# Two reorderings in the attention part of a fused attention and MLP kernel: row maxima four heads ahead instead of three, and the memory's update before its reads

## The chip, the cores and the metric

The kernel runs on one core of a Trainium2 chip. The metric is the device time of one execution in microseconds (us). Three runs of the kernel before gave 2224.09, 2224.89 and 2230.13 us; the median is 2224.89.

A core has five engines that run side by side, each in the order of its own instruction list: PE (matrix multiply; the profile shows its weight loads apart, as PEld), DVE (vector), ACT (activations and copies), POOL (GpSimd) and SP, which here does nothing but issue DMAs. An engine stands still when its next instruction waits for a semaphore, and everything behind that instruction in its list stands with it.

## The reference

The block is a conditioned residual pair: `x + ga * A(h)` with attention A, then `x + gb * B(h)` with a token-mixing MLP B. Only A matters here: 2048 rows in 4 segments of 512, 32 heads of width 32. Each segment attends to itself under a causal mask, and also reads a memory that earlier segments have filled:

```python
for s in range(N):                       # 4 segments
    qs, ks, vs = q[:, :, s], k[:, :, s], v[:, :, s]
    logits = jnp.einsum("bhqd,bhkd->bhqk", qs, ks) * scale + mask
    p = _softmax(logits, axis=-1)
    a_dot = jnp.einsum("bhqk,bhkd->bhqd", p, vs)
    pq = phi(qs)
    num = jnp.einsum("bhld,bhde->bhle", pq, M)
    den = jnp.einsum("bhld,bhd->bhl", pq, z)[..., None] + 1e-6
    o = g * (num / den) + (1.0 - g) * a_dot
    pk = phi(ks)
    M = M + jnp.einsum("bhld,bhle->bhde", pk, vs)
    z = z + jnp.einsum("bhld->bhd", pk)
```

All of it is in float32 accuracy: large products are made from operands that are split into a high and a low part, three matmuls for one.

## The kernel before, in words

**Units of work.** The attention is cut into 32 iterations t: group g of four heads, segment seg, in the order `its`: first segments 0 and 1 of every group (t = 0 to 15), then segments 2 and 3 (t = 16 to 31). An iteration has four heads h, so there are 128 heads, numbered n = 4t + h.

**The loop.** One pass of the loop at line 686 belongs to one n and records pieces of several iterations: the `scores` of head n, the row `maxima` of the head that is LEADS = 3 further on, the `values` of the head two back, and one of four pieces of `project` for the iteration two further on (LEADP = 8 heads). Into it are planned the loads and splits of the next group's weights, eight more x tiles (`token_tile`), 32 parts of the modulation matrix (`mod_fetch`, `mod_late`: a load "rawm" and one long DVE operation, L573) and wo.

**One iteration.** `project` makes k and v of the segment (matmuls `nps`, L192), transposes k (`kps`), makes q (`qps`, L200), splits k and q into high and low parts ("sg") and sends them by three small DMAs a head into that head's stack "sk" (`stack`, L374 to L376). Its last piece makes v's parts and calls `memory`. `maxima` multiplies q and k of a head (`sx`, `sy`, `sz`, L478), DVE takes the masked row maxima (L480), and for every second head PE transposes the eight columns (`nmps`, L486), ACT and DVE split them ("nt"), and four DMAs write the negated maxima of a pair of heads into rows 96 and 97 of their stacks (L493). `scores` can start only then: its matmuls `a0`, `a1`, `a2` (L515 to L522) use all 98 rows, so that the maxima are subtracted inside the product. ACT takes the exponentials (L516, L519, L523), POOL masks the diagonal blocks (L526), ACT casts a float16 part (L528), POOL makes the rest (L530), and `values` multiplies both with v (`pv`, L544). After the fourth head PE transposes the output (`ops`), ACT copies it ("ot"), and a DMA stores it ("oT").

**The memory.** `memory` (L441) reads M and z of the group (one tile MZ) in two halves: matmuls `rd` (L450), then three DVE operations (L452 to L454) that write half of tile "am". Then it makes the update: matmuls `up` (L460), DVE's masked product (L465) and POOL's sum into MZ (L466). The bank of PSUM (PE's output memory) that all these use, "ms", exists once, and `nmps` and `ops` use it too: whoever comes next waits until the one before has been read out.

**What sets the order.** The lines only record work. A scheduler of the language then places the instructions on each engine's list, after its own estimate of a timeline, within the limits of data, of buffers (banks "s1" for maxima, "s2" for scores and "pj" for projections exist twice, "pv" and "ms" once) and of `issue_after`. So a changed place in the code moves instructions nearly everywhere in the attention part. SP has one list for all DMAs, in the scheduler's order.

After the attention come the output projection (`po`, L791) and the MLP (`mx`, L921).

Of the kernel before, what the change touches and what calls it, by code (L numbers as in the profile page):

```python
# [18 lines left out]
P = 128  # L19
# [10 lines left out]
LEADP, LEADS, NSK = 8, 3, 8  # L30
# [8 lines left out]
LEADS = 3  # L39


def attention_and_mlp(ctx, tc, x, wq, wkv, wo, beta, w1, b1, w2, b2, c, wm_a, wm_b, out):
# [29 lines left out]
    def bank(tag, bufs, name):  # L72
        return psum.tile([P, 512], F32, tag=tag, bufs=bufs, name=name)
# [304 lines left out]
    def project(t, piece):  # L378
# [50 lines left out]
        else:  # L429
# [9 lines left out]
            memory(t)  # L439

    def memory(t):  # L441
        pr, g, seg = its[t]
        d = st[t]
        d["am"] = am = b.tile([P, 4, 128], F32, tag="am", bufs=3, name=f"am{t}")
        if seg:
            for half in range(2):
                ps = bank("ms", 1, f"rd{t}_{half}")[:, 0:264].rearrange("p (a n) -> p a n", a=2)
                for aa in range(2):
                    i = 2 * half + aa
                    T.matmul(ps[:, aa], d["pq"][:, 128 * i:128 * i + 128], MZ[:, g], start=True, stop=True)  # L450
                rd = b.tile([P, 2, 4], F32, tag="rd", bufs=2, name=f"rdd{t}_{half}")
                V.tensor_scalar_add(rd, ps[:, :, 128:132], 1e-6)  # L452
                V.reciprocal(rd, rd)
                V.tensor_tensor(am[:, 2 * half:2 * half + 2].rearrange("p a (h e) -> p a h e", h=4),  # L454
                                ps[:, :, 0:128].rearrange("p a (h e) -> p a h e", h=4),
                                rd.unsqueeze(3).to_broadcast([P, 2, 4, 32]), op=ALU.mult)
        if seg < 3:
            ps = bank("ms", 1, f"up{t}")
            for i in range(4):
                T.matmul(ps[:, 0:132], d["pk"][:, i], d["v32"][:, i], start=(i == 0), stop=(i == 3))  # L460
            if seg == 0:
                V.tensor_tensor(MZ[:, g], ps[:, 0:132], bdg[:, g], op=ALU.mult)
            else:
                tm = b.tile([P, 132], F32, tag="tm", bufs=1, name=f"tm{t}")
                V.tensor_tensor(tm, ps[:, 0:132], bdg[:, g], op=ALU.mult)  # L465
                G.tensor_tensor(MZ[:, g], MZ[:, g], tm, op=ALU.add)  # L466
# [126 lines left out]
    def at(f, n):  # L593
        if 0 <= n < 4 * NI:
            f(n // 4, n % 4)
# [90 lines left out]
    for n in range(-LEADS, 4 * NI + VL):  # L686
# [9 lines left out]
        if m >= 8:  # L696
            at(project, m)
        if 59 <= m < 67:
# [442 lines left out]
```

## Time and profile before

| what | us |
|---|---|
| median of three runs | 2224.89 |
| the profiled execution, its own time | 2226.6 |
| its span, first to last instruction | 2224.9 |
| PE busy in the span | 2190.3 |
| DVE / ACT / POOL busy | 1666.7 / 1135.7 / 725.8 |
| mean granted PE clock | 0.997 |

The attention loop fills about 60 to 960 us of the span, the output projection lies between 960 and 1155 us, and the MLP is the rest. A row of the profile gives line, engine, operation, the tiles written and read, and the count; then busy time, the mean of one in nanoseconds, and the idle time of that engine just before these instructions, with what ended it after the arrow. The durations of matmuls overlap with the next one's, so the step from one start to the next is the better measure of what a matmul costs PE.

### The profile page before, as it was taken

The page shows a single profiled execution, that of the slowest core. Times are in us where ns is not written, and L with a number is a line of the kernel's source. Part 1 is how long each engine was busy: PE and PEld are TensorE (multiplying, and loading weights), DVE is VectorE, ACT ScalarE, POOL GpSimd, SP SyncE. Part 2 cuts the span into 40 slices and gives each one's busy share as a digit, 9 for nine tenths or more (in the row PEclk, how much of TensorE's full clock was granted, in tenths as well). Part 3 has the DMA queues.
Part 4 walks back from the last instruction along what each step waited for, and adds up shares of the span by engine and source line. Part 5 has one row for each costly group of instructions (what it writes and reads, how often), then busy time and mean ns, then how long its engine had stood idle before and what let it go on. Part 6 is the DMA issues. An engine that isn't in the chain of part 4 may idle for free.

```text
span 2224.9 us, 38052 instructions
## 1 busy us (share of the span) xinstructions
PE 2190.3 (98%) x13786; PEld 1881.0 (85%) x13786; DVE 1666.7 (75%) x3762; ACT 1135.7 (51%) x2050; POOL 725.8 (33%) x831
## 2 busy tenths in 40 slices
PE   8999999999999999999999999999999999999999
PEld 5988898888999999888888888888888888888887
DVE  7676777756777777664858766888888886969687
ACT  5486776756666666654636533533334242424232
POOL 2175766646767776663002200033330000000000
PEclk9999999999999999999999999999999999999999
DMA  7666666686556666664754687655556542414134
GB/s 287 192 187 191 175 181 193 189 279 216 170 180 205 188 183 211 193 219 143 231 194 186 226 304 275 243 223 220 204 202 219 206 148 64 145 57 147 57 123 151
DMA packets 175183, 423.03 MB, mean 190 GB/s; under 512 B 17524, under 2 KB 71828, under 8 KB 166036
## 3 DMA queue, kind: packets, MB, share of 16 engines
q1 hardware_dynamic: 174996, 420.61, 57.5%
q8 instruction: 109, 1.79, 0.3%
q14 instruction: 78, 0.64, 0.1%
HBM read 244.62 MB, written 125.06 MB: 166 GB/s over the span
## 4 chain that ended last, share of the span: by engine, by line
PE 87%; DVE 5%; DMA 3%; ACT 2%; POOL 1%; issue 1%; SPq 0%; DVEq 0%; ACTq 0%
PE mx L921 48%; PE nps L192 11%; PE po L791 8%; PE qps L200 7%; PE pv L544 3%; PE a L515 1%; PE sz L478 1%; PE sx L478 1%; DMA sk<-nt 1%; PE up L460 1%; PE a L518 1%; POOL p L530 1%; PE a L522 1%; PE sy L478 1%; PE rd L450 1%
## 5 line engine op out<-in xcount | busy, mean ns | idle before, releaser
L921 PE MATMUL mx<-bU,sp 128*128 128x512 f32 x2352 | 534.3, 389 | 0.9 <-DVE ac L928 0.9
L921 PEld LDWEIGHTS mx<-bU,sp 128*128 128x128 f32 x2352 | 441.3, 188 | 93.4 <-issue 1.3
L119 ACT CAST sp<-wr 128x384 fp32r<-128x384 f32 (+2 forms) x408 | 218.1, 547 | 431.8 <-PE mx L921 349.1
L192 PE MATMUL nps<-wv,h 128*128 128x256 f32 x3072 | 431.2, 283 | 1.6 <-DVE h L122 0.7
L921 PE MATMUL mx<-bA,sp 128*128 128x512 f32 x1764 | 430.5, 389 | 0.0
L530 POOL TENSOR_TENSOR p<-p,ph 128x640 f16<-128x640 f32 x256 | 380.2, 1485 | 138.5 <-ACT ph L528 134.5
L192 PEld LDWEIGHTS nps<-wv,h 128*128 128x128 f32 x3072 | 400.3, 189 | 9.4 <-DVE h L122 2.0
L921 PEld LDWEIGHTS mx<-bA,sp 128*128 128x128 f32 x1764 | 331.2, 188 | 68.7
L122 DVE TENSOR_TENSOR sp<-wr,sp 128x384 fp32r<-128x384 f32 (+2 forms) x408 | 259.8, 648 | 24.7 <-ACT sp L119 24.4
L928 DVE TENSOR_TENSOR ac<-mx,ac 128x512 f32<-128x512 f32 x280 | 189.9, 687 | 85.2 <-PE mx L921 84.1
L200 PE MATMUL qps<-h,wq 128*128 128x512 f32 x768 | 197.9, 400 | 0.0
L528 ACT CAST ph<-p 128x1280 f16<-128x1280 f32 x128 | 161.4, 1261 | 59.7 <-POOL p L526 59.6
L791 PE MATMUL po<-wo,ots 128*128 128x512 f32 x768 | 180.9, 391 | 0.0
L791 PEld LDWEIGHTS po<-wo,ots 128*128 128x128 f32 x768 | 142.7, 188 | 28.7
L200 PEld LDWEIGHTS qps<-h,wq 128*128 128x128 f32 x768 | 141.6, 190 | 27.7
L921 PE MATMUL mx<-bB,sp 128*128 128x512 f32 x588 | 164.0, 389 | 0.0
L526 POOL TENSOR_SCALAR_AFFINE_SELECT p<-p 128x256 f32<-128x256 f32 x256 | 134.1, 529 | 81.8 <-ACT p L523 53.9
L921 PEld LDWEIGHTS mx<-bB,sp 128*128 128x128 f32 x588 | 110.4, 188 | 22.9
L480 DVE CUSTOM_DVE_ANT_0 sz<-sz,mask 128x512 f32<-128x512 f32 x128 | 89.1, 696 | 52.0 <-PE sz L478 49.5
L480 DVE CUSTOM_DVE_ANT_0 sx<-sx,mask 128x128 f32<-128x128 f32 (+1 forms) x256 | 93.7, 366 | 44.1 <-PE sx L478 37.9
L928 DVE TENSOR_TENSOR cc<-mx,cc 128x512 f32<-128x512 f32 x140 | 94.9, 684 | 37.6 <-PE mx L921 37.4
L516 ACT ACTIVATE p<-a,shift 128x512 f32<-128x512 f32 x128 | 88.4, 691 | 41.2 <-PE a L515 40.4
(209 smaller groups left out, 3244.7 us busy)
## 6 DMA issues: line engine op xcount, KB each, us to landing
sk<-sg SPq DMA_DIRECT2D x384, 128.0 KB
wr<-in_w_dram SPq DMA_DIRECT2D x28, 1024.0 KB
wr<-in_w_dram SPq DMA_DIRECT2D x32, 768.0 KB
bstu<-ucd SPq DMA_DIRECT2D x28, 768.0 KB
wsp<-wv SPq DMA_DIRECT2D x32, 512.0 KB
rawm<-in_wm_b_dram SPq DMA_DIRECT2D x32, 512.0 KB
wv<-wsp SPq DMA_DIRECT2D x32, 512.0 KB
pcd<-cc SPq DMA_DIRECT2D x14, 1024.0 KB
```

The costliest lines, as they stand in the source:

```text
L119: last_hi[0] = A.copy(hi, src)
L122: return lo_eng.tensor_tensor(lo, src, hi.bitcast(F32), op=ALU.subtract)
L192: T.matmul(ps[:, aa], h[:, j, 128 * tt:128 * tt + 128], wt[:, i, o:o + 256], start=(n == 0), stop=(n >= 6 * NK - 2), skip_group_check=True)
L200: T.matmul(ps, wt[:, i, o:o + 128], h[:, j], start=(k + n == 0), stop=(3 * k + n == 3 * NK - 1))
L480: marks[4 * t + h - LEADS, "V"] = V.tensor_tensor_reduce(o, o, mask[:, 384 - 128 * i:], 1.0, -3.0e38, op0=ALU.add, op1=ALU.max, accum_out= ...
L516: A.activation(p32[:, 0:512], b0, AF.Exp, scale=SCALE, bias=shift)
L526: G.affine_select(w, w, pattern=[[0, 2], [1, 128]], compare_op=ALU.is_ge, fill=0.0, base=0, channel_multiplier=-1)
L528: marks[n, "A"] = A.copy(hi, p32)
L530: marks[n, "G"] = G.tensor_tensor(lo[:, c], p32[:, c], hi[:, c], op=ALU.subtract)
L791: T.matmul(ps, os_[:, i, P * ct:P * ct + P], wop[ct, nh][:, j], start=(n == 0), stop=(n == 3 * NK - 1))
L921: T.matmul(ps, ops[q][:, i, P * k:P * k + P], b[:, j], start=(m == 0 and first), stop=(m == 3 * nk - 1), skip_group_check=True)
L928: V.tensor_tensor(d, ps, d, op=ALU.add)
```

## The change

It does three things. LEADS becomes 4: `maxima` is recorded four heads before `scores` of the same head. `memory` makes the update (matmuls and DVE product) first and the first half of the read after it, both at the old place in the last piece of `project`. The second half of the read and, behind it, POOL's sum into MZ are recorded one loop pass later, after the next iteration's first projection piece. No matmul, no vector operation and no DMA is added or removed.

```diff
--- before.py
+++ after.py
@@ -27,7 +27,7 @@
 SHIFT = 14.0 * math.log(2.0)
 NV = 97
 FT = F // P
-LEADP, LEADS, NSK = 8, 3, 8
+LEADP, LEADS, NSK = 8, 4, 8
 XB = 4
 VL = 2
 ML0 = 36
@@ -36,7 +36,7 @@
 WOS = 6
 WCT = 5
 LEADP = 8
-LEADS = 3
+LEADS = 4
 
 
 def attention_and_mlp(ctx, tc, x, wq, wkv, wo, beta, w1, b1, w2, b2, c, wm_a, wm_b, out):
@@ -436,34 +436,49 @@
             V.tensor_tensor(r1, v, vp[:, :, :, 1:33], op=ALU.subtract)
             A.copy(vp[:, :, :, 33:65], r1)
             V.tensor_tensor(vp[:, :, :, 65:97], r1, vp[:, :, :, 33:65], op=ALU.subtract)
-            memory(t)
-
-    def memory(t):
+            memory(t, 0)
+
+    def read(t, half):
         pr, g, seg = its[t]
         d = st[t]
-        d["am"] = am = b.tile([P, 4, 128], F32, tag="am", bufs=3, name=f"am{t}")
-        if seg:
-            for half in range(2):
-                ps = bank("ms", 1, f"rd{t}_{half}")[:, 0:264].rearrange("p (a n) -> p a n", a=2)
-                for aa in range(2):
-                    i = 2 * half + aa
-                    T.matmul(ps[:, aa], d["pq"][:, 128 * i:128 * i + 128], MZ[:, g], start=True, stop=True)
-                rd = b.tile([P, 2, 4], F32, tag="rd", bufs=2, name=f"rdd{t}_{half}")
-                V.tensor_scalar_add(rd, ps[:, :, 128:132], 1e-6)
-                V.reciprocal(rd, rd)
-                V.tensor_tensor(am[:, 2 * half:2 * half + 2].rearrange("p a (h e) -> p a h e", h=4),
-                                ps[:, :, 0:128].rearrange("p a (h e) -> p a h e", h=4),
-                                rd.unsqueeze(3).to_broadcast([P, 2, 4, 32]), op=ALU.mult)
-        if seg < 3:
-            ps = bank("ms", 1, f"up{t}")
-            for i in range(4):
-                T.matmul(ps[:, 0:132], d["pk"][:, i], d["v32"][:, i], start=(i == 0), stop=(i == 3))
-            if seg == 0:
-                V.tensor_tensor(MZ[:, g], ps[:, 0:132], bdg[:, g], op=ALU.mult)
-            else:
-                tm = b.tile([P, 132], F32, tag="tm", bufs=1, name=f"tm{t}")
-                V.tensor_tensor(tm, ps[:, 0:132], bdg[:, g], op=ALU.mult)
-                G.tensor_tensor(MZ[:, g], MZ[:, g], tm, op=ALU.add)
+        ps = bank("ms", 1, f"rd{t}_{half}")[:, 0:264].rearrange("p (a n) -> p a n", a=2)
+        for aa in range(2):
+            i = 2 * half + aa
+            T.matmul(ps[:, aa], d["pq"][:, 128 * i:128 * i + 128], MZ[:, g], start=True, stop=True)
+        rd = b.tile([P, 2, 4], F32, tag="rd", bufs=2, name=f"rdd{t}_{half}")
+        V.tensor_scalar_add(rd, ps[:, :, 128:132], 1e-6)
+        V.reciprocal(rd, rd)
+        V.tensor_tensor(d["am"][:, 2 * half:2 * half + 2].rearrange("p a (h e) -> p a h e", h=4),
+                        ps[:, :, 0:128].rearrange("p a (h e) -> p a h e", h=4),
+                        rd.unsqueeze(3).to_broadcast([P, 2, 4, 32]), op=ALU.mult)
+
+    def update(t):
+        pr, g, seg = its[t]
+        d = st[t]
+        ps = bank("ms", 1, f"up{t}")
+        for i in range(4):
+            T.matmul(ps[:, 0:132], d["pk"][:, i], d["v32"][:, i], start=(i == 0), stop=(i == 3))
+        if seg == 0:
+            V.tensor_tensor(MZ[:, g], ps[:, 0:132], bdg[:, g], op=ALU.mult)
+        else:
+            d["tm"] = tm = b.tile([P, 132], F32, tag="tm", bufs=1, name=f"tm{t}")
+            V.tensor_tensor(tm, ps[:, 0:132], bdg[:, g], op=ALU.mult)
+
+    def memory(t, step):
+
+
+        pr, g, seg = its[t]
+        d = st[t]
+        if step == 0:
+            d["am"] = b.tile([P, 4, 128], F32, tag="am", bufs=3, name=f"am{t}")
+            if seg < 3:
+                update(t)
+            if seg:
+                read(t, 0)
+        elif seg:
+            read(t, 1)
+            if seg < 3:
+                G.tensor_tensor(MZ[:, g], MZ[:, g], d["tm"], op=ALU.add)
 
     def maxima(t, h):
         d = st[t]
@@ -695,6 +710,8 @@
                     load_w(its[t][1], its[t][0])
         if m >= 8:
             at(project, m)
+        if m % 4 == 0 and 0 < m <= 4 * NI:
+            memory(m // 4 - 1, 1)
         if 59 <= m < 67:
             seg, ct = 2 + (m - 59) // 4, 2 * ((m - 59) % 4)
             with ExitStack() as s:
```

The scheduler's order moves with it. Three places are shown; in the names the number behind a tile is the iteration, then the head or half, and the last is a buffer number.

The first is PE's list in iteration 13, before: from the second half of the read (`rd13_1`) to the update (`up13`) on the same bank. `nps14` are projections of the next iteration, and `pv` rows, of which there are a few between, are left out.

```order
L450 MATMUL rd13_1_6481<-MZ_127,pq13_6383 128x132 x2
...
L192 MATMUL nps14_0_6575<-wv0_7_1_1_6402,h0_7_451 128x256 x6
L192 MATMUL nps14_1_6692<-wv0_7_1_1_6402,h0_6_423 128x256 x5
L192 MATMUL nps14_1_6692<-wv0_7_1_1_6402,h0_7_451 128x256 x6
L478 MATMUL sy_13_1_6765<-sk1_1_502 128x384
L478 MATMUL sz_13_1_6768<-sk1_1_502 128x512
L521 MATMUL a2_12_0_6516<-sk0_0_497 128x128
L522 MATMUL a2_12_0_6516<-sk0_0_497 128x256
L515 MATMUL a0_12_1_6631<-sk0_1_498 128x512
L460 MATMUL up13_6488<-v32_13_6066,pk13_6388 128x132 x4
```

The same place with the change; the update stands further up, and here the bank goes from the first half of the read to the second.

```order
L447 MATMUL rd13_0_6502<-MZ_127,pq13_6395 128x132 x2
...
L192 MATMUL nps14_0_6579<-wv0_7_1_1_6414,h0_6_423 128x256 x4
L192 MATMUL nps14_0_6579<-wv0_7_1_1_6414,h0_7_451 128x256 x6
L192 MATMUL nps14_1_6713<-wv0_7_1_0_6411,h0_4_367 128x256 x2
L192 MATMUL nps14_1_6713<-wv0_7_1_0_6411,h0_5_395 128x256 x6
L192 MATMUL nps14_1_6713<-wv0_7_1_1_6414,h0_6_423 128x256 x6
L192 MATMUL nps14_1_6713<-wv0_7_1_1_6414,h0_7_451 128x256 x4
...
L493 MATMUL sy_13_2_6787<-sk1_2_503 128x384
L405 MATMUL kps14_6819<-ident_90,k32_14_6576 128x128 x2
L447 MATMUL rd13_1_6630<-MZ_127,pq13_6395 128x132 x2
```

Between the two holders of the bank there were 17 projection matmuls and some of the scores and maxima; now there are 30 (28 in the rows, two in a gap), and scores and maxima again.

The second place is SP's list where iteration 20 sends its stacks, before. `sg20` rows fill the stack of head 0 (L374, L375, L376 in this order), `nt` rows carry maxima of iteration 19's heads 0 and 1.

```order
L374 DMA sk0_0_497<-sg20_9501 32x2x512
L375 DMA sk0_0_497<-sg20_9501 32x2x512
L493 DMA sk1_0_501<-nt0_19_1_9467 1x4x128
L493 DMA sk1_0_501<-nt1_19_1_9468 1x4x128
L493 DMA sk1_1_502<-nt0_19_1_9467 1x4x128
L493 DMA sk1_1_502<-nt1_19_1_9468 1x4x128
L376 DMA sk0_0_497<-sg20_9501 32x1024
```

With the change (L508 is the old L493):

```order
L508 DMA sk1_0_501<-nt0_19_1_9364 1x4x128
L508 DMA sk1_0_501<-nt1_19_1_9365 1x4x128
L508 DMA sk1_1_502<-nt0_19_1_9364 1x4x128
L508 DMA sk1_1_502<-nt1_19_1_9365 1x4x128
...
L577 DMA oT_57<-ot17_9403 128x512
L374 DMA sk0_0_497<-sg20_9513 32x2x512
L375 DMA sk0_0_497<-sg20_9513 32x2x512
L376 DMA sk0_0_497<-sg20_9513 32x1024
```

The four small DMAs with maxima stood between the second and the third DMA of head 0's stack; they stand ahead of all three now, and the store `oT` is the last ahead of them.

The third place is PE's list in iteration 5 to 7, before: scores of iteration 5 (`a0_5_3` and so on) and maxima of iteration 7 with projections `nps8` between them.

```order
L515 MATMUL a0_5_3_3602<-sk1_3_504 128x512
L192 MATMUL nps8_1_3882<-wv0_4_0_0_3317,h0_0_254 128x256 x6
L192 MATMUL nps8_1_3882<-wv0_4_0_0_3317,h0_1_275 128x256 x6
L192 MATMUL nps8_1_3882<-wv0_4_0_1_3320,h0_2_311 128x256 x6
L518 MATMUL a1_5_3_3605<-sk1_3_504 128x384
L192 MATMUL nps8_1_3882<-wv0_4_0_1_3320,h0_3_339 128x256 x5
L521 MATMUL a2_5_3_3608<-sk1_3_504 128x128
L522 MATMUL a2_5_3_3608<-sk1_3_504 128x256
```

With the change, from the last scores matmul of iteration 5's head 2; the next row is that head's `pv5_2`:

```order
L537 MATMUL a2_5_2_3505<-sk1_2_503 128x256
L460 MATMUL up7_3687<-v32_7_3276,pk7_3595 128x132 x4
L493 MATMUL sy_7_1_3853<-sk1_1_502 128x384
L530 MATMUL a0_5_3_3614<-sk1_3_504 128x512
L533 MATMUL a1_5_3_3617<-sk1_3_504 128x384
L493 MATMUL sz_7_1_3856<-sk1_1_502 128x512
L447 MATMUL rd7_0_3694<-MZ_127,pq7_3590 128x132 x2
L536 MATMUL a2_5_3_3620<-sk1_3_504 128x128
L537 MATMUL a2_5_3_3620<-sk1_3_504 128x256
L530 MATMUL a0_6_0_3715<-sk0_0_497 128x512
L533 MATMUL a1_6_0_3718<-sk0_0_497 128x384
L447 MATMUL rd7_1_3822<-MZ_127,pq7_3590 128x132 x2
```

In this stretch stands no projection: the update, both reads, maxima and the scores of two heads follow each other directly.

## The prediction

> **What bounds the kernel now.** First the page's busy times, then the same by stretch of the span (PE, PEld, DVE, ACT, POOL busy, then granted clock, DMA share and GB/s), for the attention loop.
>
> ```profile
> PE 2190.3 (98%) x13786; PEld 1881.0 (85%) x13786; DVE 1666.7 (75%) x3762; ACT 1135.7 (51%) x2050; POOL 725.8 (33%) x831
> ...
> 60.00:130.00 70.00, 68.80 (x539) 63.18 (x539) 46.33 (x148) 37.22 (x74) 21.18 (x27) 1.00 0.57 176
> 130.00:560.00 430.00, 416.00 (x3680) 380.42 (x3679) 307.83 (x887) 303.28 (x554) 272.08 (x314) 0.98 0.68 203
> 560.00:960.00 400.00, 395.42 (x3561) 363.73 (x3560) 289.28 (x881) 255.34 (x443) 276.37 (x331) 1.00 0.64 193
> ```
>
> PE is the bound, and in the loop it stands for only 1.2 + 14.0 + 4.6 = 19.8 us. The change adds no matmul, so its gain is bounded by these pauses and by what a lowered clock costs, which the middle row shows as 0.98. Next, who PE waited for between 130 and 960 us (total, times, longest), the rows that the change can touch.
>
> ```profile
> PE a L515 <- DMA sk<-nt: 4.1, 5, 1.4
> PE up L460 <- DVE am L454: 3.8, 3, 3.5
> PE sy L478 <- DVE mx L480: 1.9, 2, 1.2
> ...
> PE sx L478 <- DMA sk<-sg: 0.2, 1, 0.2
> ```
>
> The first two are what the two halves of the change act on: scores waiting for the row maxima, and the update waiting until the read's second half has left the bank. One wait makes up nearly all of the second row. Here it is on PE's timeline, and below it what DVE did meanwhile.
>
> ```profile
> 451.42 0.40 PE L515 MATMUL a<-sk 98*128 98x512 f32 x1
> 455.29 2.10 PE L460 MATMUL up<-v,pk 128*128 128x132 f32 x8 [3.48 <-DVE am L454]
> ```
>
> ```profile
> 447.83 0.13 DVE L480 DVE_READ_ACCUMULATOR2_ANT mx<- 128x1 f32 x1
> 449.51 1.92 DVE L573 SCALAR_TENSOR_TENSOR rawm<-rawm,scb 128x1024 f32<-128x1024 f32 x1 [1.55 <-DMA rawm<-in_wm_b_dram]
> 451.36 0.08 DVE L573 DVE_READ_ACCUMULATOR rawm<-rawm,scb 128x1 f32 x1
> 451.36 2.69 DVE L122 TENSOR_TENSOR wq<-rawq,wq 128x512 fp32r<-128x512 f32 x2
> ...
> 454.73 0.41 DVE L454 TENSOR_TENSOR am<-rd,rdd 128x256 f32<-128x256 f32 x1
> ```
>
> DVE waited 1.55 us for a late transfer, then worked through the long modulation operation and two weight splits before it came to the read (iteration 13). From 447.96 to 455.14 are 7.2 us. The stall has an aftermath, in the clock column of the second of these stretches; the first two stretches show a smaller case, to which I come back.
>
> ```profile
> 130.00:133.00 3.00, 2.22 (x12) 1.37 (x10) 2.71 (x7) 3.00 (x6) 1.12 (x4) 1.00 1.01 233
> 133.00:137.00 4.00, 4.00 (x28) 3.79 (x28) 3.36 (x4) 4.00 (x8) 3.73 (x3) 0.58 1.08 253
> ...
> 454.00:464.00 10.00, 8.71 (x45) 7.83 (x46) 7.53 (x26) 4.31 (x9) 4.33 (x9) 0.50 0.99 371
> ```
>
> For ten microseconds PE ran at half its clock: 10 x 0.5 = 5.0 us lost beside the 3.48 us of standing. This one place costs 8.5 us, 0.38% of the kernel.
>
> **The change part by part.** To compare orders I laid the rows of both orders of PE's list end to end, each at its step in the trace. The next rows give the step of a projection matmul, (478.04 - 475.60) / 20 = 0.122 us, and of `a0`, 0.24 us; other steps are read off in the same way. PE work between two instructions, the cover, hides a chain on other engines that is shorter.
>
> ```profile
> 475.60 2.60 PE L192 MATMUL nps<-wv,h 128*128 128x256 f32 x20
> 478.04 0.39 PE L515 MATMUL a<-sk 98*128 98x512 f32 x1
> 478.28 0.34 PE L518 MATMUL a<-sk 98*128 98x384 f32 x1
> ```
>
> *Update first, in iteration 13.* The bank's next holder after the stalled DVE stretch is now `rd13_1`. From the last maxima product ahead of it (`sz13_1`) PE has 14 projections, two scores and half a `pv` up to the first read, 2.5 us, then 30 projections (3.7 us) and 1.2 us of others: 7.4 us of cover. DVE's list has the same operations between, after that maxima's own 0.8 us: 8.0 us if the transfer is as late as before. The wait falls from 3.48 to 0.6 us (0 if the load is on time, 3.5 if another operation slips in): **-2.9**. A wait of 0.6 us should leave the clock alone: **-5.0**, between 0 and -5.0. DVE is not faster; its delay is covered, and what comes late next are the results of the read, which `values` needs only some seven heads later.
>
> [...] The row of 133 to 137 us disagrees: the clock fell to 0.58 after a stretch in which PE was busy 2.22 of 3 us, with waits of at most 0.65 us. [...]
>
> So a pile-up of short waits can cost (1 - 0.58) x 4 = 1.7 us, a price that a rival below uses.
>
> *Maxima a head earlier, the scores' side.* The wait of 4.1 us came in five places. Its chain is `nmps`, two short operations and the small DMAs. Cover from `nmps` to the first scores of the pair: before, 27 of 64 pairs have under 8 us, the least 3.2; with the change 10 have, the least 5.0, and the median goes from 9.3 to 11.6. In proportion 10/27 x 4.1 = 1.5 us remain: **-2.6**, between 0 and -4.1.
>
> *Maxima a head earlier, their own side.* What the scores gain in distance the maxima lose: `sx` of an iteration's first head comes at the median 7.5 us of PE work after `qps`, before 11.4. Between lie the splits, three DMAs and their landing. Two instances, SP's rows for iterations 22 and 20 behind the last `qps` matmul of each on PE, and from the chain that ended last the time of such a transfer:
>
> ```profile
> 698.04 0.51 PE L200 MATMUL qps<-h,wq 128*128 128x512 f32 x1
> ...
> 700.72 0.56 SPq L376 DMA_DIRECT2D sk<-sg  x1
> ```
>
> ```profile
> 639.93 0.71 PE L200 MATMUL qps<-h,wq 128*128 128x512 f32 x2
> ...
> 643.78 1.22 SPq L375 DMA_DIRECT2D sk<-sg  x1
> 645.10 2.64 SPq L493 DMA_DIRECT2D sk<-nt  x4
> 647.78 0.58 SPq L376 DMA_DIRECT2D sk<-sg  x1
> ...
> 129.27 3.26 DMA sk<-sg
> ```
>
> Undisturbed, the third DMA is issued 700.72 - 698.55 = 2.2 us after `qps` and landed 3.3 us later: 5.5 us. With four `nt` issues of 2.64 us and others in front it was issued at 7.1 and ready at 10.4 us, still within that iteration's 12.2 us of cover. In the new order the `nt` issues stand ahead of the stack's, mostly for maxima transposed 1 to 7 us before `qps` ends. So I take 5.5 us plus, in odd iterations, some 1 us for the store `oT` between. Only four early iterations fall below 6.5 us of cover (9 with 4.7, 7 with 5.6, 13 with 5.7, 3 with 6.2): **+1.0**. If the queue stays as disturbed as it was, it is much more: a rival.
>
> *Places where PE runs out of projections.* Scores, exponentials and `pv` of one head form a chain; these rows give its links.
>
> ```profile
> L526 POOL TENSOR_SCALAR_AFFINE_SELECT p<-p 128x256 f32<-128x256 f32 x256 | 134.1, 529 | 81.8 <-ACT p L523 53.9 <-ACT p L519 27.1
> L528 ACT CAST ph<-p 128x1280 f16<-128x1280 f32 x128 | 161.4, 1261 | 59.7 <-POOL p L526 59.6
> ...
> L523 ACT ACTIVATE p<-a,shift 128x384 f32<-128x384 f32 x128 | 74.7, 583 | 57.3 <-PE a L522 55.6 <-PE pv L544 0.8
> ```
>
> From `a2` to `pv` pass at least 0.58 + 2 x 0.53 + 1.26 = 2.9 us. Before, the smallest cover there is 4.0 us. With the change three heads have less: `pv1_0` 1.2, `pv5_2` 2.5 (the third order shown) and `pv7_0` 2.6 us, and at the same places a bank of scores comes round after 0.3 us where its exponential takes 0.58. Missing are 1.7 + 0.4 + 0.3, partly in place of waits that stand there already:
>
> ```profile
> 129.55 0.33 PE L521 MATMUL a<-sk 98*128 98x128 f32 x1 [0.65 <-ACT p L516]
> ...
> 131.02 0.51 PE L515 MATMUL a<-sk 98*128 98x512 f32 x1 [0.52 <-ACT p L519]
> ```
>
> Net I take **+2.0**; it can be 0, or 7 if all that falls short of its chain in the new order (10 us, before 5, the maxima's banks among it) adds up without overlap.
>
> *The rest.* POOL's sum into MZ a head later delays nobody: after segment 1 the same MZ is next used 15 iterations later, and after segment 2 the next segment's read is recorded three heads behind the sum. The 132-column products are the same in number. From 960 us on PE was busy throughout and its list is the same from `po8` on: 0.
>
> **Sum**: -2.9 - 5.0 - 2.6 + 1.0 + 2.0 = -7.5 us. Against the profiled execution's 2226.6 us this is 2219.1; that execution lay 1.7 us above the median of 2224.89, so I forecast 2217.4, rounded to 2217 us, 0.35% below. Within 0.3%, some 6.7 us, a measurement of this kernel can hardly tell from no change.
>
> **The rivals.** *The stacks arrive late (slower).* Decides when the third DMA of head 0 is issued more than 7.5 - 3.3 = 4.2 us after `qps`. With the `nt` issues still in its way it is ready at 2.2 + 2.6 + 3.3 = 8.1 us, and each of 31 iterations stands 0.6 us at its first maxima: +19 in place of +1, 2235 us. For it: iteration 20 above took 7.1 us to that issue, without harm only because nobody was waiting yet. Against: the order shown, with the `nt` issues moved ahead. *The clock falls all the same.* The pile-up at `pv1_0`, or a second wait behind DVE's late load, lowers it once for ten microseconds: +5.0, 2222 us; two short falls give +3.4, 2220. For it: the 133 us row. Against: nothing of 3 us is left in the covers. *The change moves the wait and does nothing.* The late load meets another bank instead of "ms", say `pv11_3` right behind `rd13_1`: +7.9, 2225 us. For it: DVE's list is in order and as full as before. *All goes well.* No pile-up costs anything, the scores' wait and the short fall at 133 us (1.7) go entirely: -2.9 - 5.0 - 4.1 - 0.6 - 1.7 = -14.3, 2211 us.
>
> **How the numbers follow.** Forecast with its own range 2212 to 2221: 0.40. Late stacks: 0.30. Clock falls or wait moves: 0.20. All goes well: 0.10. The range takes in the forecast, the good case with 4 us below it and the late stacks with 3 us above them, for waits that no row of before names: 2207 to 2238, with about 2 in 10 outside. Faster by over 0.3% (below 2218.2): two thirds of the forecast, the good case and a sixth of the clock's, 0.40. Slower by over 0.3% (above 2231.6): most of the late stacks, and a little of the rest, 0.30. Within: the remaining 0.30.
>
> **What would show it.** In the profile after: no wait of more than 1 us before `rd` or `up` near 450 us and a clock of 1.00 in that stretch (first steps); under 2 us of waits of `a0` for `sk<-nt`; under 2 us of `sx` for `sk<-sg`, else the late stacks are right; short waits of `a`, `sx` and `pv` near 125, 250 and 300 us and the clock there. The forecast is wrong if waits for DMA or DVE in the loop exceed their 19.8 us, or if the clock falls twice.

## The result, and the profile after

The changed kernel takes 2249.53 us (median of five runs, 2241.73 to 2251.98); five runs of the kernel before beside it gave 2225.77 (2224.09 to 2230.13). The ratio is 1.0101, 95% interval [1.008, 1.0122]: **slower by about 23 us**, where 2217 and a range up to 2238 were forecast. The profiled execution's own time is 2249.53 us, its span 2247.8, its mean clock 0.994.

First PE's busy time on the page, then the same stretches as before (PE, PEld, DVE, ACT, POOL busy, granted clock, DMA share, GB/s).

```profile
PE 2202.1 (98%) x13786; PEld 1887.5 (84%) x13786; DVE 1672.1 (74%) x3762; ACT 1133.6 (50%) x2050; POOL 721.1 (32%) x831
```

```profile
60.00:130.00 70.00, 68.33 (x533) 62.36 (x534) 46.24 (x146) 33.22 (x67) 18.48 (x24) 1.00 0.55 170
130.00:560.00 430.00, 406.86 (x3529) 368.48 (x3529) 305.54 (x864) 300.90 (x546) 265.80 (x305) 0.97 0.66 195
560.00:960.00 400.00, 394.71 (x3558) 362.64 (x3555) 284.27 (x870) 253.73 (x442) 273.65 (x334) 1.00 0.63 192
```

The loss lies in the middle row: between 130 and 560 us PE stands 23.1 us where it stood 14.0, and got through 3529 matmuls where it got through 3680. From 560 us on little is lost, and the MLP takes what it took (1072.5 us from its first product, before 1071.6). Who PE waited for between 130 and 960 us:

```profile
PE sx L493 <- DMA sk<-sg: 8.1, 6, 4.6
PE a L530 <- DMA sk<-nt: 3.9, 1, 3.9
PE sx L493 <- DMA gaw<-in_x_dram: 1.7, 1, 1.7
PE nmps L501 <- DVE am L451: 1.7, 2, 1.5
PE kps L405 <- ACT k L398: 1.7, 3, 0.9
```

The 3.5 us of `up` behind `am` are gone, as forecast. In their place the maxima wait for their stacks: with the pause at 960.5 us it is 10.2 us, which before cost 0.2. The 1.7 us named `gaw` are such a wait too: iteration 3's first stack landed at 145.81 us, 0.14 us before `sx` began. The longest of these pauses, on PE's list and then on SP's list:

```profile
422.29 0.47 PE L493 MATMUL sz<-sk 96*128 96x512 f32 x1
427.41 0.77 PE L493 MATMUL sx<-sk 96*128 96x128 f32 x2 [4.64 <-DMA sk<-sg]
```

```profile
417.12 0.43 SPq L681 DMA_DIRECT2D gaw<-in_x_dram  x1
417.64 0.61 SPq L374 DMA_DIRECT2D sk<-sg  x1
418.30 0.59 SPq L375 DMA_DIRECT2D sk<-sg  x1
418.94 0.58 SPq L376 DMA_DIRECT2D sk<-sg  x1
419.57 0.58 SPq L150 DMA_DIRECT2D rawv<-in_wkv_dram  x1
420.26 2.12 SPq L508 DMA_DIRECT2D sk<-nt  x3
423.97 0.68 SPq L374 DMA_DIRECT2D sk<-sg  x1
425.04 0.64 SPq L375 DMA_DIRECT2D sk<-sg  x1
426.65 0.56 SPq L376 DMA_DIRECT2D sk<-sg  x1
```

This `sx`, of the second head of iteration 12, waits for the three DMAs issued at 417.64, 418.30 and 418.94 us. They were issued one right behind the other and landed at 425.02, 426.64 and 427.27 us, 7.4 to 8.3 us after their issue; PE went on at 427.41. So here the landing was late and not the issue. The prediction had put 3.3 us on such a landing. Over the 31 iterations from the second on, the third DMA of the first head's stack takes 2.4 us to land at the median in both kernels, and 8.9 us before and 9.6 us after at the most. While the late three were under way the DMA engines were busy for 0.88 of the time (the column before the last); that this made them late is likely, not shown.

```profile
416.00:424.00 8.00, 6.76 (x65) 6.08 (x63) 4.10 (x16) 4.25 (x8) 6.00 (x9) 1.00 0.88 210
```

The next stack, issued at 423.97 to 426.65 us, shows a second delay, of the issue. SP's own waits between 415 and 428 us name what held it:

```profile
SPq L374 <- DMA gaw<-in_x_dram: 1.5, 1, 1.5
SPq L376 <- DMA sk<-sg: 1.0, 1, 1.0
```

Each of these three was issued right after the transfer eight places ahead in SP's list had landed: at 423.97 after the `gaw` load (issued 417.12, landed 423.91), then at 425.04 and 426.65 after the first two DMAs of the late stack (425.02 and 426.64). The other long pause comes from SP's list too: `gaw<-modd` waits 7.1 us for the row it reads to be stored, and the four `nt` DMAs stand behind it in the list, in the following rows SP's list, its wait, and PE.

```profile
508.68 1.08 SPq L601 DMA_DIRECT2D modd<-mrow  x1
516.96 0.34 SPq L624 DMA_DIRECT2D gaw<-modd  x1
517.40 2.62 SPq L508 DMA_DIRECT2D sk<-nt  x4
```

```profile
SPq L624 <- DMA modd<-mrow: 7.1, 1, 7.1
```

```profile
520.26 0.50 PE L530 MATMUL a<-sk 98*128 98x512 f32 x1 [3.91 <-DMA sk<-nt]
```

The clock is the other half. Short stretches of the same columns, each pause with what followed it:

```profile
130.00:134.00 4.00, 2.73 (x12) 1.48 (x11) 2.63 (x11) 4.00 (x8) 1.63 (x2) 1.00 0.19 53
134.00:142.00 8.00, 5.70 (x29) 4.64 (x28) 5.66 (x7) 6.68 (x13) 5.76 (x7) 0.57 0.99 263
...
424.00:432.00 8.00, 4.59 (x21) 4.53 (x21) 1.65 (x6) 2.31 (x3) 1.01 (x1) 0.57 0.66 164
448.00:456.00 8.00, 6.44 (x74) 5.53 (x72) 4.40 (x18) 8.00 (x19) 4.95 (x5) 0.98 0.60 166
456.00:462.00 6.00, 5.51 (x24) 5.00 (x24) 3.30 (x8) 3.81 (x6) 4.87 (x6) 0.50 1.06 295
512.00:520.00 8.00, 4.35 (x47) 3.90 (x45) 4.23 (x14) 6.03 (x11) 3.92 (x5) 1.00 0.65 258
520.00:524.00 4.00, 3.74 (x17) 3.63 (x18) 2.54 (x6) 2.35 (x3) 1.01 (x2) 0.57 0.60 161
957.00:961.00 4.00, 1.87 (x20) 1.73 (x19) 0.29 (x1) 1.55 (x3) 3.12 (x4) 0.98 0.80 174
961.00:965.00 4.00, 4.00 (x31) 3.90 (x31) 3.00 (x12) 1.84 (x2) 0.98 (x5) 0.59 0.59 127
```

Five times the clock fell to half, for 27.3 us before the MLP in all; before it fell twice, for 13.7 us. Up to the MLP's first product PE stood 31.4 us after its first 60 (before 19.8), and that product came 22.1 us later.

### The profile page after: what moved, and what is told of

It is laid out like the page before. It is cut to its first block, busy times and chain, and to the rows that moved or that the text cites. A ratio compares the mean times of both kernels' runs of the same rounds, so it can differ in the third digit from the quotient of the medians.

```text
span 2247.8 us, 38004 instructions
## 1 busy us (share of the span) xinstructions
PE 2202.1 (98%) x13786; PEld 1887.5 (84%) x13786; DVE 1672.1 (74%) x3762; ACT 1133.6 (50%) x2050; POOL 721.1 (32%) x831
## 4 chain that ended last, share of the span: by engine, by line
PE 84%; DVE 6%; DMA 4%; ACT 3%; POOL 2%; issue 1%; SPq 0%; ACTq 0%; DVEq 0%; POOLq 0%
PE mx L938 46%; PE nps L192 11%; PE po L808 8%; PE qps L200 6%; PE pv L559 3%; DMA sk<-sg 1%; POOL p L545 1%; PE sx L493 1%; ACT ph L543 1%; PE a L530 1%; PE sz L493 1%; PE sy L493 1%; PE a L533 1%; PE rd L447 1%; PE srow L294 1%
## 5 line engine op out<-in xcount | busy, mean ns | idle before, releaser
L541 POOL TENSOR_SCALAR_AFFINE_SELECT p<-p 128x256 f32<-128x256 f32 x256 | 127.8, 502 | 101.8 <-ACT p L538 60.1
L538 ACT ACTIVATE p<-a,shift 128x384 f32<-128x384 f32 x128 | 74.2, 580 | 61.2 <-PE a L537 59.6
```

The source lines that it names most:

```text
L538: A.activation(p32[:, 896:1280], b2_[:, 0:384], AF.Exp, scale=SCALE, bias=shift)
L541: G.affine_select(w, w, pattern=[[0, 2], [1, 128]], compare_op=ALU.is_ge, fill=0.0, base=0, channel_multiplier=-1)
```

## The experiments

I held at first **Q** (lead 4 brings the maxima too close behind their stacks) against **M** (the memory's new order costs, by short waits of its own). Later came **R** (S in the first expectations): the scheduler draws the whole order anew at any edit, and one order is better or worse than another whatever the edit was for. All ratios are to the kernel before on the same chip.

**The memory alone, and the lead alone.** Edit of the changed kernel in the first (in both places where it is set), of the kernel before in the second:

```diff
-LEADP, LEADS, NSK = 8, 4, 8
+LEADP, LEADS, NSK = 8, 3, 8
```

```diff
-LEADP, LEADS, NSK = 8, 3, 8
+LEADP, LEADS, NSK = 8, 4, 8
```

> The change's memory half alone: update first, second half of the read a head later, LEADS back at 3. Theory Q (the slowdown comes from the maxima reaching the stacks before SP's queue has delivered them): the waits of sx for sk<-sg fall from 10.2 us to under 1 us, and the time is near before, 2216 to 2229 us. Theory M (the memory half packs update and reads into stretches without projections, and that costs): it stays slow, 2240 to 2252 us. Theory S (any reordering of this tuned list costs some 20 us by chance): 2235 to 2255, with the waits spread over many causes.

> The change's other half alone: LEADS 4, memory as before. Theory Q: slow like the change, 2238 to 2255 us, with 8 us or more of sx waiting for sk<-sg and at least 20 us at half clock. Theory M: near before, 2216 to 2232 us, whatever the waits of sx. Theory S: slow, but with under 4 us of sx waiting for sk<-sg.

Measured: 2240.13 us, ratio 1.0052 [1.0036, 1.0068] for the memory; 2237.05 us, 1.0041 [1.0027, 1.0056] for the lead. Taken by themselves these runs split the loss in half. The reshuffled orders below show that this reading was wrong.

**The update first alone.** Lead 3, both halves of the read and POOL's sum at the old place, only the update ahead of them.

```diff
-        elif seg:
-            read(t, 1)
-            if seg < 3:
-                G.tensor_tensor(MZ[:, g], MZ[:, g], d["tm"], op=ALU.add)
+                read(t, 1)
+                if seg < 3:
+                    G.tensor_tensor(MZ[:, g], MZ[:, g], d["tm"], op=ALU.add)
```

> LEADS 3, update first, but both halves of the read and the sum at the old place. Theory Q: 2216 to 2230 us. Theory M: if the order update before read is what costs, 2238 to 2252; if only the later second half costs, near before. Theory S: anything within 15 us of the change.

Measured 2231.82 us, ratio 1.0017 [1.0006, 1.0028]. The waits of `sx` for the stacks between 130 and 960 us are long here too, although the lead is 3:

```profile
PE sx L492 <- DMA sk<-sg: 6.5, 6, 1.8
```

**Lead 5.** The changed kernel with LEADS = 5.

> A larger dose: the change with LEADS 5 in place of 4, so that an iteration's first maxima are recorded one pass behind the DMAs of its stacks. Theory Q: the waits of sx for sk<-sg grow beyond 30 us in total, the waits of a0 for sk<-nt fall further, and the time is over 2270 us. Theories M and S: like the change, 2240 to 2258 us.

Measured 2262.59 us, ratio 1.0159 [1.0139, 1.0179]. The time follows the dose (lead 3, 4, 5 with the new memory, one order each: 2240, 2250, 2263), but the waits for the stacks do not: 6.8 us at lead 5, where Q asked for over 30. From `qps` to the first maxima pass 8.4 us at the median in this trace and 7.5 us in that of lead 4, so by this measure, waits and half clock included, the distance shrinks no further. What grew is half clock, 44.4 us in nine falls, behind pauses of `a`, `pv`, `sx` and `sy` of 0.5 to 2.6 us. Why the fifth head does that was not tested.

**Edits that mean nothing.** To see how much of a time is the order and not the change, two exchanges of lines that change no work: the loops around the four `nt` DMAs, and the copies of k and v out of their bank. Each was made in the kernel before and in the changed kernel.

```diff
-        for hh in range(2):
-            sk = d["sk", h - 1 + hh]
-            for part in range(2):
+        for part in range(2):
+            for hh in range(2):
+                sk = d["sk", h - 1 + hh]
```

```diff
-            A.copy(k32[:, 2 * half:2 * half + 2], ps[:, :, 0:128])
             A.copy(v32[:, 2 * half:2 * half + 2, 0:128], ps[:, :, 128:256])
+            A.copy(k32[:, 2 * half:2 * half + 2], ps[:, :, 0:128])
```

> The kernel before, with the two loops round the four small nt DMAs of a pair of heads exchanged (hi of both heads, then lo of both): the same work, lead 3, the old memory; it only makes the scheduler interleave everything behind head 2 otherwise. Theory Q (what the change costs belongs to the change: shorter distance from the stacks to the maxima, reads in two places): nothing of the change is here, so the time stays within 0.3% of the kernel before (2219 to 2232 us), idle time of the loop near 20 us, half clock near 14. Theory R (the order before is a lucky one; any edit that reshuffles the scheduler's interleaving loses its fits): 2232 to 2245 us with new waits at sx for sk<-sg and at pv, idle 25 to 30 us, and no edit of the change needed for it.

> The kernel before, with the two copies of k and v out of the projection's bank recorded in the other order: same work, lead 3, old memory, another reshuffling of the order, from head 0 on. Theory Q: within 0.3% of the kernel before (2219 to 2232 us). Theory R: 2232 to 2245 us, idle 25 to 30 us in the loop, waits scattered over sx, pv, a and nps.

> The changed kernel with the same exchange of the nt DMAs' loops. Theory Q: the cost goes with lead 4 and the split read, so 2243 to 2256 us (within 0.3% of the changed kernel), with waits of sx for sk<-sg of 8 to 12 us again and half clock of 20 to 30 us. Theory R: the places change, and with them the sum: anywhere from 2230 to 2255 us, more likely below 2249 than above; the 4.6 us at sx_12_1 and the 3.9 us at a0_14_0 are gone and others are there.

> The changed kernel with the copies of k and v in the other order. Theory Q: 2243 to 2256 us, as for the exchange of the DMAs. Theory R: 2230 to 2255 us, and if the two reshuffled changed kernels lie more than 0.4% apart from each other or from 2249, the size of the loss is mostly that of the draw.

Measured: the kernel before 2229.2 us, 0.9999 [0.9982, 1.0017], and 2231.98, 1.0015 [1.0002, 1.0028]. The changed kernel 2240.32, 1.006 [1.0039, 1.0081], and 2236.65, 1.0039 [1.0025, 1.0052]. So 9 to 14 of the 23 us came with this one order of the changed kernel, and the rest stays in both others. What stays shows in PE's waits between 130 and 960 us, first the two orders of the kernel before, then the two of the changed kernel:

```profile
PE sx L478 <- DMA sk<-sg: 0.7, 1, 0.7
```

```profile
PE sx L478 <- DMA sk<-sg: 3.1, 3, 1.4
```

```profile
PE sx L493 <- DMA sk<-sg: 7.4, 9, 1.7
```

```profile
PE sx L493 <- DMA sk<-sg: 8.6, 8, 1.9
```

Three orders before: 0.2, 0.7 and 3.1 us. Three orders of the change: 8.1, 7.4 and 8.6 us. Such waits are not lead 4's alone: with lead 3, the two kernels with the update first above have 4.6 and 6.5 us.

**The memory's second half alone, and both memories in another order.** Lead 3 throughout; the first has the read's first half ahead of the update as before and only the second half later:

```diff
-            if seg < 3:
-                update(t)
             if seg:
                 read(t, 0)
+            if seg < 3:
+                update(t)
```

> Lead 3, the memory in before's order (first half of the read, then the update) but with the second half of the read and POOL's sum a head later: the half of the memory's change that is left when the update first is taken out. The distance from the stacks to the first maxima is as before (median 11.5 us of PE work), the least distance of head 0 from maxima to scores falls from 19.5 to 14.7 us. Theory Q (late stacks from lead 4): this does not touch it, so sx for sk<-sg stays under 3.5 us as in the three kernels with lead 3 and the old memory, and the time is 2225 to 2236 us. Theory M (the read in two places is what costs, by short waits on DVE and ACT): 2236 to 2242 us, as the whole of the new memory with lead 3 gave (2240).

> The kernel with only the read's second half a head later (lead 3), and the copies of k and v recorded in the other order, which does no other work but makes the scheduler order everything anew. Theory L (the late second half is a gain by its mechanism: two reads and an update no longer follow each other through the one bank, with idle time near 13 us): 2210 to 2221 us again. Theory R (that gain was a lucky draw): 2222 to 2236 us, with waits of 20 us or more in the loop.

> The kernel with the whole new memory (update first and read late, lead 3), with the copies of k and v exchanged. Theory U (the update first costs: the first half of the read has to wait until DVE has emptied the bank of the update, and stands later): 2234 to 2246 us again. Theory R (2240 was an unlucky draw; update first is worth nothing either way): 2212 to 2230 us.

Measured: the late half alone 2214.25 us, 0.9934 [0.9916, 0.9952], and with k and v exchanged 2222.33, 0.9978 [0.9967, 0.9989]. The whole new memory with k and v exchanged: 2223.57, 0.9981 [0.9972, 0.9991], where the first order of the same gave 2240. M falls, and so does the split in halves: the new memory costs +12 us in one order and gains 4 in another. The late half gained in both its orders, 14 and 5 us (the first is faster than Q or M had it), which makes a real gain likely but is two draws only. In the first the clock never falls in the loop and PE stands least of the eight kernels with lead 3, as its two stretches show:

```profile
130.00:560.00 430.00, 419.64 (x3780) 386.85 (x3779) 316.10 (x915) 311.34 (x566) 280.29 (x322) 1.00 0.69 205
560.00:960.00 400.00, 399.65 (x3586) 366.84 (x3585) 291.93 (x893) 256.88 (x444) 282.22 (x337) 1.00 0.64 192
```

**The lead alone in two more orders.** The two exchanges in the kernel before with LEADS = 4.

> The kernel before with lead 4 alone, copies of k and v exchanged: from qps to the first maxima 7.0 us of PE work at the median, least 3.8 (before 11.4 and 4.3). Theory Q (the distance costs, whatever the order): waits of sx for sk<-sg of 4 to 9 us, 2233 to 2246 us. Theory R (only the draw): 2222 to 2233 us, waits of sx anywhere from 0 to 5 us.

> The kernel before with lead 4 alone, the nt DMAs' loops exchanged: 7.0 us of PE work at the median from qps to the first maxima, least 3.2. Theory Q: waits of sx for sk<-sg of 4 to 9 us, 2233 to 2246 us. Theory R: 2222 to 2233 us. If one of the two orders lies on each side, the mean of the three (this, the other and 2237) against that of the three orders of the kernel before (2226, 2229, 2232) is what the lead costs, within some 5 us.

Measured 2252.71 us, 1.012 [1.0087, 1.0154], slower than Q or R had it, and 2237.59, 1.0039 [1.0024, 1.0053]. With the first that is three orders of lead 4 alone at ratios of 1.0041, 1.012 and 1.0039, mean 1.0067. Three orders of the whole change: 1.0101, 1.006, 1.0039, mean 1.0067. Three of the kernel before, itself as 1: mean 1.0005; two of the new memory with lead 3: 1.0052 and 0.9981, mean 1.0017. **On average the lead costs about 0.6%, 14 us, and no cost of the memory's new order is seen.** Three orders are few where they spread over 0.8%, so here are all: the six kernels with lead 4 above lie between 1.0039 and 1.012, mean 1.0067; the eight with lead 3, with the memory old, new or in part new, between 0.9934 and 1.0052, mean 0.9997. The difference is 0.7%, 95% interval 0.3 to 1.1%. The waits of `sx` for the stacks in the three orders of the lead alone are 5.6, 5.2 and 5.3 us (7.5 for the last over the whole loop).

**The stacks on another list.** In the changed kernel the three DMAs of each iteration's first head are issued by ACT, from iteration 2 on.

```diff
-        SY.dma_start(skf[0:32], src[:, 0:3:2])
-        SY.dma_start(skf[32:64], src[:, 0:4:3])
-        last_sk[t, h] = SY.dma_start(skf[64:96], src[:, 1:3])
+        Q = SY if h or t < 2 else A
+        Q.dma_start(skf[0:32], src[:, 0:3:2])
+        Q.dma_start(skf[32:64], src[:, 0:4:3])
+        last_sk[t, h] = Q.dma_start(skf[64:96], src[:, 1:3])
```

> The changed kernel with the three stack DMAs of each iteration's first head issued by ACT instead of SP: no other transfer stands in front of them in a list, the distance to the first maxima is as short as in the changed kernel (median 7.7, least 2.9 us). Theory Q in its form 'SP's list holds them': sx for sk<-sg at head 0 falls under 3 us, the time to 2234 to 2243 (ACT has 93 more issues, which may give 2 to 5 us back). Theory D (full DMA engines make the landing late): these waits stay at 6 us or more. Theory 'the splits on DVE are late': the waits stay too, and the releaser's issue comes right behind DVE's split of q.

Measured 2268.25 us, 1.0172 [1.0154, 1.0191], against the form of Q that blames SP's list alone. PE's waits between 130 and 960 us, and one instance on ACT's list and on PE's:

```profile
PE sx L494 <- DMA sk<-sg: 13.4, 6, 3.7
PE a L537 <- ACT p L532: 6.2, 3, 5.1
```

```profile
327.73 0.63 ACTq L375 DMA_DIRECT2D sk<-sg  x1
...
329.33 0.59 ACTq L376 DMA_DIRECT2D sk<-sg  x1
...
329.98 0.84 ACTq L377 DMA_DIRECT2D sk<-sg  x1
```

```profile
336.22 0.50 PE L494 MATMUL sx<-sk 96*128 96x128 f32 x2 [3.29 <-DMA sk<-sg]
```

The last of these three was issued 3.1 us after `qps` and was still 6.2 us under way. Over the 31 iterations from the second on, the third DMA is issued 2.9 us after `qps` at the median, and 3.9 us in the changed kernel, but it takes 4.2 us to land where it took 2.4, and is there 7.5 us after `qps` where it was there after 6.5. Why it lands later is not shown. Nor did the edit free the stacks from other transfers: a DMA on ACT's list now stood until a transfer of SP's list had landed (it was issued at 506.79 us, the one before it at 502.20), as a stack on SP's list had stood for the `gaw` load. The 5.1 us that PE waits for an exponential (second row) are this case:

```profile
502.20 0.59 ACTq L376 DMA_DIRECT2D sk<-sg  x1
506.79 0.57 ACTq L377 DMA_DIRECT2D sk<-sg  x1
507.40 0.69 ACT L532 ACTIVATE p<-a,shift 128x512 f32<-128x512 f32 x1 [6.82 <-DMA h<-hT]
```

The DMA at 506.79 us was issued only after the `h` load eight places ahead, both lists taken together, had landed, at 506.71, and the exponential behind it waited with it.

**The distance given back.** LEADP becomes 9: every projection a head earlier, so that lead 4 leaves the maxima as far behind `qps` as before. The fourth stack is sent with the next projection's first piece, since its tile is still read, and the plan of weights moves along.

```diff
-LEADP, LEADS, NSK = 8, 4, 8
+LEADP, LEADS, NSK = 9, 4, 8
...
-            for h in range(3):
+            for h in range(2):
                 stack(t, h)
         else:
-            stack(t, 3)
+            stack(t, 2)
...
+        if m % 4 == 0 and 8 < m <= 4 * NI:
+            stack(m // 4 - 1, 3)
```

It was run with the whole change, with the old memory, with the change and k and v exchanged, and with the change less its update first.

> The changed kernel with the projections a head earlier too (LEADP 9; the fourth stack then goes with the next projection, so that nobody overwrites scores still to be read): from the end of qps to the first maxima of an iteration PE again has 11.5 us of work at the median and never under 9.9 (changed kernel 7.5 and 4.7; before 11.4 and 4.3). Theory Q: the waits of sx for sk<-sg fall from 7 to 10 us to under 3, and the time by 8 to 15 us, to 2225 to 2241. Theory D (the transfers themselves are late, because the DMA engines are full, whatever the distance): the waits stay above 6 us and the time at 2240 or more. Theory R alone (luck of the order): waits of sx need not fall, time anywhere from 2230 to 2250.

> Lead 4 and the projections a head earlier with the old memory: from qps to the first maxima 11.3 us of PE work at the median and never under 7.6, from nmps to the scores 11.4 and never under 6.8 (before 11.4 and 4.3; 9.3 and 3.2). If the two distances are what the waits depend on, both the waits of a for sk<-nt (4.1 before) and of sx for sk<-sg fall under 1.5 us, and the time is 2215 to 2226 us, which would be the fastest here; theory R gives 2225 to 2240, since the order is drawn anew; theory D gives waits of sx of 5 us or more.

> The changed kernel with the projections a head earlier, copies of k and v exchanged. Theory Q (distance): the least distance from qps to the first maxima is 6.0 us in this order and 9.9 in the one that took 2210, the median the same 11.5; waits of sx for sk<-sg 3 to 5 us, time 2207 to 2218. Theory R: 2218 to 2235.

> Lead 4, the projections a head earlier, the read's second half a head later, but the first half of the read ahead of the update as in the kernel before. Theory U (update first costs, 26 us between two of the kernels with lead 3): 2195 to 2207 us, the fastest so far. Theory L without U: within 0.3% of the 2210 us with the update first (2203 to 2217). Theory R: 2205 to 2230.

Measured: 2210.06 us, **0.9909 [0.9893, 0.9926]**, the fastest of all; 2229.46, 1.0003 [0.9992, 1.0014]; 2226.0, 0.9988 [0.9976, 0.9999]; 2224.99, 0.9987 [0.9977, 0.9996]. The mean of the four is 0.9972, against 1.0067 for the six kernels with lead 4 and LEADP 8. The slowest of the four lies 0.36% below the fastest of those six, so the loss is gone. The distance is back too: from the landing of the first head's stack to its first maxima pass 1.1 to 1.3 us at the median in the six, 3.8 to 4.3 us in the four, and 2.9 to 4.7 us in the eight with lead 3. But the waits for the stacks fell less than Q asked (3.3, 5.3, 5.3 and 4.5 us between 130 and 960 us). With the old memory they hardly fell at all, from 5.6, 5.2 and 5.3 us with lead 4 alone, while the time fell by 0.6%:

```profile
PE sx L478 <- DMA sk<-sg: 5.3, 4, 2.3
```

So it is not shown that the gain comes by these waits. The last three of the four also lie where R had them, and not where Q, U or L did. And no run has the projections a head earlier with lead 3, so they may gain by themselves and not by the distance. The 2210 us is partly a good draw: the same kernel with two copies exchanged takes 16 us more. In the fastest the second half of the loop runs with only 0.4 us of gaps:

```profile
560.00:960.00 400.00, 399.64 (x3597) 368.38 (x3595) 285.14 (x895) 257.48 (x446) 280.76 (x338) 1.00 0.64 193
```

## Why the prediction was wrong, point by point

**The failed step is "their own side", +1.0.** It took the third DMA to be issued 2.2 us after `qps` and landed 3.3 us later, 5.5 us against 7.5 us of cover. The 2.2 us were the least of all 31 iterations, in both kernels: the median is 4.2 us before and 3.9 after, with a quarter above 6.3 and 4.9. Nor were the 3.3 us a quiet landing: they are iteration 3's, at a DMA share of 1.02 (129.27 to 132.53 us), and the median is 2.4 us, with single ones up to 9.6. So in the changed kernel this DMA had landed 6.5 us after `qps` at the median, in a quarter of the iterations after more than 8.1 us, at the latest after 17.0, against the same 7.5 us of cover. About 1 us of slack was left in the median iteration, where the kernel before had 2.9, and in 8 of the 31 `sx` began within 0.15 us of the landing. Instead of 1.0 us the waits for stacks took 10.2 us in seven pauses, two of them at a later head of the iteration, which the sum had not looked at.

The rival of the late stacks had the mechanism, and a decision point (issue later than 4.2 us) that the kernel before already met in half of its iterations: 0.30 was too low a chance for it. Two rows picked by hand stood for a distribution that the trace had in full. Nor did "the `nt` issues moved ahead" free the list: the median issue came only 0.2 us earlier. The rival's price of 0.6 us in each of 31 iterations was wrong in form, since the delays came bunched, with the clock behind them.

**Update first, -2.9: right.** No wait behind `am` of 0.5 us or more is left near 450 us. But both reshuffled orders of the kernel before lost that pause too (and had others of 2.9 and 3.2 us near 494), so it belonged to that order more than to the code. **Its clock, -5.0: wrong.** The clock fell at the same place for another 6.8 us, after `sx13_0` had waited 1.56 us, and four times elsewhere. That a wait of 0.6 us leaves the clock alone was the author's estimate, and the two kernels' traces show no length of wait up to which it does: in the kernel before 1.36 us (at 939.84) brought no fall, while the one at 132.98 us came behind waits of at most 0.65 us; in the changed kernel 1.74 us (at 145.95) brought none and the 1.56 us did. In all 27.3 us ran at half clock where it had been 13.7, which is some 6.8 us lost where 5.0 were to be gained.

**Scores' wait, -2.6: right as a tendency.** It fell to 1.6, 2.9 and 1.0 us in the three orders of lead 4 alone and to 2.1 in one other order of the change; in the third the waits name none. But the other two orders of the kernel before had 2.0 and 3.1 us themselves, so the mean of three falls from 3.1 to 1.8 us, half of what was forecast. In the changed kernel one pause of 3.9 us took it all back, behind the modulation's round trip, which the sum had not looked at.

**Pile-ups, +2.0: right in place, too low.** From 129.5 to 139 us PE waited 4.0 us in seven pauses (before 1.4 in three), and 6.8 us of half clock followed (3.4). Behind `up7` (269.6 us), where `pv5_2` and then `pv7_0` come, no wait of `pv` is above 0.3 us up to 326 us.

**The rest, 0: right.** Nobody waited for POOL's sum, and from the MLP's start on the difference is 0.9 us.

**What the sum could not hold.** It priced named places and left the others as they were, in an order that is drawn anew. Identical work in other orders differs by 16 us (2240 and 2224, 2210 and 2226), twice the gain that was summed to a tenth of a microsecond. Of the 23 us measured, by the means above, some 14 are the lead's own and some 9 the draw's.

Over the 20 profiled executions of this study one line fits the start of the MLP to 2.9 us (standard deviation): 1121.6 us + 1.29 for each microsecond that PE stands after 60 us + 0.43 for each microsecond at half clock (standard errors 0.15 and 0.08). Averaged over three orders each, the change adds 6.4 us of standing (27.7 for 21.3) and 9.1 us of half clock (20.5 for 11.4): 8.2 + 3.9 = 12.1 us, and 11.3 were measured at that point. The waits of `sx` that the traces put down to the stacks make 7.4 us of it (8.7 for 1.3, whole loop); all others together shrank by 1.0 us, where the sum had them shrink by 3.5 (-2.9 - 2.6 + 2.0). **Open** stays why lead 4 alone, with only 4.7 us more of waits for stacks than its three neighbours before, stands 7.9 us longer.

## What to carry to other kernels

A distance between two steps of a pipeline has two ends: before lengthening one, take the whole distribution of the delay at the other end, issue and landing of every instance, and compare its median and upper quarter with the cover that is left. Where a scheduler orders the lists, run the kernel with one or two meaningless exchanges first; the spread of those is the size below which a sum of named waits predicts little, and a part of a change is judged by the mean over several orders. Here moving the consumer a head earlier lost some 14 us on average, and the loss was gone once the producer was moved a head earlier as well.

## What the runs showed of the hardware

- DMAs hold each other up in this program: SP issues 1256 in each of the traces before and after, and none before the one eight places ahead had landed (423.97 after 423.91, 425.04 after 425.02, 426.65 after 426.64). With ACT issuing some of them, one of its own followed such a landing too (506.79 after 506.71). So one late landing delayed an issue that has nothing to do with it: the `gaw` load's held the next stack for 1.5 us.
- A transfer of the same size landed after 2.4 us at the median and after 9.6 us at the most in the changed kernel, 7.4 to 8.3 us in the longest pause. Issued from ACT's list it took 4.2 us at the median.
- The clock fell also after stretches in which PE was partly busy: 1.87 of 4 us before 961 us, 2.73 of 4 before 134. The falls in the two kernels' traces last 3.41 us or a multiple of it (3.41 and 10.24 before; 6.83 three times and 3.41 twice after), apart from the last record of a trace. So the pause of 2.13 us at 960.5, with a fall of 3.41 us behind it, cost 1.7 us of clock more, half of 3.41. The fit's 1.29 has each microsecond of standing cost 0.3 beside, twice its standard error; what this 0.3 is made of is not shown.
